# Moving the tail clears, the scatters, a table and the rank products of a fused attention, dense and routed kernel to other slots

## The chip, the cores and the metric

The kernel runs on one core of a Trainium2 chip. The metric is the device time of one execution in microseconds; three executions of the kernel before took 601.76, 603.11 and 604.13 us, median 603.11 us. One further execution was recorded by the hardware profiler, and all rows below come from it.

## What is computed

Three stages follow each other; the second and third work on 3072 tokens of 256 values.

```python
# 1. chunked linear attention, 4 x 8 heads, 768 positions, head 32, state 16
y[:, :, sl] = y_intra + y_inter
# 2. dense layer 256 -> 2048 -> 256 with a leaky relu per hidden column
h = x @ w_in
g = np.maximum(h, 0.0) + alpha * np.minimum(h, 0.0)
x = g @ w_out
# 3. eight experts 256 -> 1024 -> 256, the best one of each token
logits = x @ w_gate + modality_bias[modality_id]
e_idx = np.argmax(logits, axis=1)
for e in range(E):
    mask = e_idx == e
    h = np.maximum(x[mask] @ w1[e], 0.0)
    out[mask] = gate_w[mask, None] * (h @ w2[e])
```

## The kernel before

The tokens are cut into nine blocks of 2 or 3 chunks of 128 (`SIZES`). Attention makes the input of a block, the dense layer takes it through 16 units of 128 hidden columns, and routing sends its rows to their experts: they are scattered into a table `srt` in DRAM that has one stretch of rows for each expert. The expert stage then takes 14 items; an item is one page of 256 rows of one expert (`xr`, read from `srt`) with that expert's weights (four loads of 512 KB, `raw`).

From block 3 on the work is written out by hand in **slots**, under `manual_schedule`, so that each engine takes its instructions in the order in which the slots issue them. Blocks 3 to 8 have 16 slots each, then each item has 8. `at[k, f]` is the slot of unit f of block k, and `ui` is the first slot of item 0, which comes right behind slot 15 of block 8, the last block. In slot u PE makes the first product of unit u (`ph`, six matmuls), ACT and DVE make `t` and `g` from it, ACT and POOL split the `g` of slot u-1 into `gh` and `gl` (L616, L618), and PE makes the second product (`px`) of the unit of slot u-4 (`LAG`), which needs that unit's `gh` and `gl`. `g` has three buffers, the PSUM tile `ph` three. The table `todo` hangs everything else on slots with `do(slot, function)`:

- **Routing** of a block, `route_at`: `route_mm` and `route_act` (logits and rows, `pxr`, `xr`), `route_b`, `route_exp`, `route_gate`, `route_c` (the ranks of the tokens within their experts, products `pr` on PE) and `route_d` (L553: adds the running count `cnt`, makes the row numbers `pi`, and issues one indirect DMA for each chunk, L569, on POOL's queue: the **scatter**). For blocks 0 to 2 `pr` lies in one of the three `ph` tiles.
- **Tails**: `tail_counts` (L1012) copies `cnt` to `cnti` on DVE and calls `clear_tails` (L457): eight DMAs on SP's queue, one for each expert, each writes 640 empty rows of 1032 bytes behind the expert's last row so far, 8 x 660 KB in all. Only the last block's scatters are told to come behind them (L576 to L578); scatters of other blocks lie behind nothing, since no clear stands ahead of them in the program.
- **Tables**: `item_tables` (L716 to L742 and above) works out which item has which expert and page, on DVE, in four steps of a slot each. Table 0 serves items 0 and 1, table 1 (`tab_194`) items 2 to 8, table 2 the rest. `item_load` reads the table and loads the weights, `item_rows` loads the page behind all scatters and clears so far; both issue on SP's queue, in program order.

A scheduler adds the semaphores: an instruction waits for the earlier ones whose data it reads or overwrites, unless `declare_no_dep` says that two don't meet. A scatter writes to rows that only data tells, so it counts as a write to the whole of `srt`.

Of the kernel before, what the change touches and what calls it, by code (L numbers as in the profile page):

```python
# [112 lines left out]
def ssm_moe_moe_kernel(  # L113
# [26 lines left out]
    blocks = [(sum(SIZES[:k]), n) for k, n in enumerate(SIZES)]  # L140
# [57 lines left out]
    blk = {}  # L198
# [160 lines left out]
    m2p = []  # L359
# [189 lines left out]
    def wait_for(i, o, why):  # L549
        tc.add_manual_dep(i, o.name, mybir.DependencyInfo(mybir.DependencyClass.Sync, mybir.DependencyReason.DATA),  # L550
                          reason=why)

    def route_d(k):  # L553
        c0, n = blocks[k]
        d = blk[k]
        pr, oh, xr = d["pr"], d["oh"], d["xr"]
        sh = [P, n, NE]
        V = nc.vector

        q = small.tile([P, MX, NE], F32, tag="q", name="q")  # L560
        V.tensor_tensor(q[:, :n], pr[:, :n], cnt[:, None, :].to_broadcast(sh), ALU.add)
        V.tensor_tensor(cnt, pr[:, n], cnt, ALU.add)
        V.tensor_tensor(q[:, :n], q[:, :n], oh[:, :n], ALU.mult)
        pf = small.tile([P, MX], F32, tag="pf", name="pf")
        V.tensor_reduce(pf[:, :n], q[:, :n], AX.X, ALU.add)
        pi = small.tile([P, MX], I32, tag="pi", name="pi")
        V.tensor_copy(pi[:, :n], pf[:, :n])
        for t in range(n):
            sc = nc.gpsimd.indirect_dma_start(  # L569
                out=srt[:, :], out_offset=bass.IndirectOffsetOnAxis(ap=pi[:, t:t + 1].bitcast(U32), axis=0),  # L570
                in_=xr[:, t, :ROW], in_offset=None, bounds_check=NROW - 1, oob_is_err=False)

            for o in scat:
                tc.declare_no_dep(sc.ins, o, reason="rows are disjoint")
            scat.append(sc.ins)
            if k == len(blocks) - 1:  # L576
                for o in tails:
                    wait_for(sc.ins, o, "rows behind the last ones")  # L578
# [366 lines left out]
    split_load(1)  # L945
    for step in (route_a, route_b, route_exp, route_gate, route_c, route_d):
        step(0)

    last = len(blocks) - 1
    slots = [("m",) + q for q in late] + [("i", i, fc) for i in range(NSTATIC) for fc in range(KF2)]
    at = {q[1:]: u for u, q in reversed(list(enumerate(slots))) if q[0] == "m"}
    ui = len(late)
# [3 lines left out]
    def do(u, fn, *args):  # L958
        todo.setdefault(u, []).append((fn, args))
# [65 lines left out]
    def route_at(k, mms, b):  # L1025
        for t, u in enumerate(mms):
            do(u, route_mm, k, t)
            do(u + 1, route_act, k, t)
        for v, fn in zip(b, (route_b, route_exp, route_gate, route_c, route_d)):
            do(v, fn, k)  # L1030

    u = at[NS, 0]
    route_at(1, (u, u + 1), (u + 4, u + 5, u + 6, u + 6, u + 8))
    route_at(2, (u + 5, u + 7), (u + 9, u + 10, u + 11, u + 11, u + 14))
    for k in range(NS, last + 1):
        u = at[k, 15] + 1
        if k < last - 1:
# [4 lines left out]
    def table_at(u, j, pool):  # L1042
        steps = []

        def step():
            if not steps:
                steps.append(item_tables(j, pool[-1]))
            next(steps[0], None)

        for v in range(u, u + 5):  # L1050
            do(v, step)

    table_at(at[last - 1, 14], 0, small_)
    table_at(at[last, 11], 1, m2p)
    do(ui, tail_counts)
    table_at(ui + 12, 2, m2p)

    for k in range(NS, last):
        c0, n = blocks[k + 1]
# [3 lines left out]
        for j in range(n):  # L1063
            c, b = c0 + j, at[k, 0] + 5 * j - (k > NS)
# [30 lines left out]
    for i in range(2, NSTATIC):  # L1095
        b = ui + KF2 * (i - 2)
# [109 lines left out]
```

## Time and profile before

| | us |
|---|---|
| median of three executions | 603.11 |
| the profiled execution | 600.14 |
| its span from first to last instruction | 598.3 |
| PE busy in the span | 549.2 (92%) |
| DVE busy | 437.9 (73%) |
| ACT busy | 319.0 (53%) |
| POOL busy | 242.0 (40%) |
| mean granted TensorE clock | 0.95 of 2.4 GHz |

PE is busy all through most 15 us windows; the windows in which it isn't are the start (up to 180 us, where blocks 0 to 2 run with their attention) and two around the change from the dense layer to the items, 405 to 450 us. Idle time of another engine counts only where PE waits for it. A row of the timeline gives the start in us, the length in us, engine and line, the operation with its tiles, how many were merged, and in brackets the idle time before it and what ended that.

### The profile page before, as it was taken

The numbers are of one execution on the slowest core, as the hardware profiler recorded it, in microseconds if no ns is written. First come the engines' busy times: TensorE is split into PE (matmuls) and PEld (weight loads), VectorE is DVE, ScalarE is ACT, GpSimd is POOL, SyncE is SP. The second block draws the span as 40 slices with busy tenths as digits, with TensorE's granted clock in tenths as the row PEclk, the third lists the DMA queues.
The fourth block names the chain that finished last, engine by engine and source line by source line (L and its number), as shares of the span: only waits on it lengthen the run. The fifth ranks groups of instructions, "written<-read, shape, count | busy, mean of one in ns | idle before, by whom it ended". The sixth has DMA issues, their size and how long they took to land. (4 is left out here: it accounts for less than half of the span.)

```text
span 598.3 us, 12098 instructions
## 1 busy us (share of the span) xinstructions
PE 549.2 (92%) x4271; PEld 515.5 (86%) x4271; DVE 437.9 (73%) x861; ACT 319.0 (53%) x702; POOL 242.0 (40%) x258
## 2 busy tenths in 40 slices
PE   7988785999879999989999999997959999999993
PEld 7867575799768899979999999997959999999993
DVE  4998797963787777778766777488549777877860
ACT  0563664565564354464444444564537677767761
POOL 1143353655435654845845746454004122211211
PEclk9785797999999999999999999997979999999998
DMA  7977654520145226225234200631997976777400
GB/s 231 285 256 222 208 179 148 167 89 1 36 135 171 96 85 182 78 86 180 92 101 145 84 24 22 204 134 35 276 315 248 331 242 218 214 233 230 144 25 7
DMA packets 60563, 92.15 MB, mean 154 GB/s; under 512 B 5102, under 2 KB 37040, under 8 KB 60496
## 3 DMA queue, kind: packets, MB, share of 16 engines
q1 hardware_dynamic: 56974, 82.83, 44.3%
q0 software_dynamic: 2400, 6.32, 2.9%
q10 hardware_dynamic: 1122, 2.16, 1.3%
q8 instruction: 36, 0.59, 0.4%
q14 instruction: 31, 0.25, 0.2%
HBM read 75.59 MB, written 15.96 MB: 153 GB/s over the span
## 5 line engine op out<-in xcount | busy, mean ns | idle before, releaser
L618 POOL TENSOR_TENSOR gl<-g,gh 128x384 fp32r<-128x384 f32 (+1 forms) x144 | 146.8, 1023 | 147.0 <-ACT gh L616 144.6
L607 ACT ACTIVATE t<-ph,sgn 128x384 f32<-128x384 f32 (+1 forms) x144 | 78.5, 546 | 121.2 <-PE ph L153 105.2
L609 DVE SCALAR_TENSOR_TENSOR g<-ph,sal,t 128x384 f32<-128x384 f32 (+1 forms) x144 | 81.1, 566 | 69.8 <-ACT t L607 69.0
L153 PE MATMUL ph<-xh,wi_h 128*128 128x384 f32 (+1 forms) x288 | 100.0, 349 | 14.6 <-DVE g L609 14.4
L153 PE MATMUL px<-gl,wo_h 128*128 128x384 f32 (+1 forms) x288 | 94.9, 330 | 1.7 <-POOL gl L618 1.7
L153 PE MATMUL px<-gh,wo_h 128*128 128x384 f32 (+1 forms) x288 | 94.6, 329 | 1.8 <-ACT wo_h L424 1.4
L153 PE MATMUL px<-gh,wo_l 128*128 128x384 f32 (+1 forms) x288 | 94.0, 327 | 0.0
L153 PE MATMUL ph<-xl,wi_h 128*128 128x384 f32 (+1 forms) x288 | 93.1, 324 | 0.3 <-DVE xl L159 0.3
L153 PE MATMUL ph<-xh,wi_l 128*128 128x384 f32 (+1 forms) x288 | 93.0, 323 | 0.0
L616 ACT CAST gh<-g 128x384 fp32r<-128x384 f32 (+1 forms) x144 | 67.4, 469 | 17.3 <-DVE g L609 17.1
L877 POOL DMA_INDIRECT out_dram<-ob,xr x26 | 28.1, 1080 | 111.3 <-ACT ob L876 65.9
L153 PEld LDWEIGHTS ph<-xh,wi_h 128*128 128x128 f32 x288 | 55.6, 194 | 19.9 <-DVE g L609 16.7
L854 ACT ACTIVATE rh<-ph 128x256 fp32r<-128x256 f32 (+1 forms) x112 | 41.6, 371 | 54.0 <-PE ph L153 53.2
L855 DVE SCALAR_TENSOR_TENSOR rl<-ph,rh 128x256 fp32r<-128x256 f32 (+1 forms) x112 | 45.2, 403 | 23.5 <-ACT rh L854 22.5
L153 PEld LDWEIGHTS px<-gl,wo_h 128*128 128x128 f32 x288 | 56.4, 196 | 3.2 <-POOL gl L618 2.1
L153 PEld LDWEIGHTS px<-gh,wo_h 128*128 128x128 f32 x288 | 56.7, 197 | 2.3 <-ACT wo_h L424 1.6
L153 PEld LDWEIGHTS px<-gh,wo_l 128*128 128x128 f32 x288 | 56.5, 197 | 0.2 <-DVE wo_l L159 0.2
L153 PEld LDWEIGHTS ph<-xl,wi_h 128*128 128x128 f32 x288 | 55.9, 194 | 0.8 <-DVE xl L159 0.5
L153 PEld LDWEIGHTS ph<-xh,wi_l 128*128 128x128 f32 x288 | 55.8, 194 | 0.0
L153 PE MATMUL ph<-x2h,wi_h 128*128 128x256 f32 x144 | 41.7, 290 | 5.6 <-DVE rl L855 5.6
L964 DVE TENSOR_TENSOR_SCAN ab<-ab,id 128x512 f32<-128x512 f32 x30 | 44.2, 1475 | 0.0
L569 POOL DMA_INDIRECT srt<-xr,pi x24 | 25.7, 1072 | 43.5 <-DVE sets L695 30.5
(149 smaller groups left out, 1306.5 us busy)
## 6 DMA issues: line engine op xcount, KB each, us to landing
raw<-in_w_dram SPq DMA_DIRECT2D x56, 512.0 KB
ab<-a_scr SPq DMA_DIRECT2D x24, 512.0 KB
srt<-zr SPq DMA_DIRECT2D x8, 645.0 KB
raw<-in_w_in_dram SPq DMA_DIRECT2D x8, 512.0 KB
raw<-in_w_out_dram SPq DMA_DIRECT2D x8, 512.0 KB
bs<-bcs SPq DMA_DIRECT2D x38, 96.0 KB
bs<-bcs SPq DMA_DIRECT2D x19, 192.0 KB
xr<-srt SPq DMA_DIRECT2D x14, 258.0 KB
```

The lines of the kernel that those rows point to most:

```text
L153: nc.tensor.matmul(o, l, r, start=start, stop=stop)
L569: sc = nc.gpsimd.indirect_dma_start(out=srt[:, :], out_offset=bass.IndirectOffsetOnAxis(ap=pi[:, t:t + 1].bitcast(U32), axis=0), in_=xr[:, ...
L607: nc.scalar.activation(t[:, :N], ph[:, :N], AF.Copy, scale=sg)
L609: nc.vector.scalar_tensor_tensor(g[:, :N], ph[:, :N], sal[:, fc:fc + 1], t[:, :N], ALU.mult, ALU.max)
L616: nc.scalar.copy(gh[:, :N], g[:, :N])
L618: nc.gpsimd.tensor_tensor(gl[:, :N], g[:, :N], f(gh[:, :N]), ALU.subtract)
L854: nc.scalar.activation(rh[:, :n], ph[:, :n], AF.Relu)
L855: nc.vector.scalar_tensor_tensor(rl[:, :n], ph[:, :n], 0.0, f(rh[:, :n]), ALU.max, ALU.subtract)
L877: nc.gpsimd.indirect_dma_start(out=out[:, :], out_offset=bass.IndirectOffsetOnAxis(ap=xr[:, t, ROW - 1:ROW].bitcast(U32), axis=0), in_=ob, ...
L964: nc.vector.tensor_tensor_scan(lt[:, s_].rearrange("p h i -> p (h i)"), lt[:, s_].rearrange("p h i -> p (h i)"), id8[:, s_].rearrange("p h ...
```

## The change

- `route_d` no longer issues the scatters. They are a function of their own, `route_out(k, ts)`. For blocks 1 to 7 the scatters of a block are issued one a slot, in the three (or two) slots behind `route_d`; for block 8 in `route_d`'s own slot, as before. Block 0's all go out at once, as before.
- `tail_counts` moves from slot `ui` to slot `at[8, 11]`, five slots earlier. In that slot it is issued behind the first scatter of block 7, and ahead of the other two (slots 12 and 13).
- Table 1 starts at `at[8, 13]` and not at `at[8, 11]`.
- For blocks 1 and 2 `route_c` comes a slot later, `route_d` too.

```diff
-        for t in range(n):
+        d["pi"] = pi
+
+    def route_out(k, ts):
+        pi, xr = blk[k]["pi"], blk[k]["xr"]
+        for t in ts:
             sc = nc.gpsimd.indirect_dma_start(
                 out=srt[:, :], out_offset=bass.IndirectOffsetOnAxis(ap=pi[:, t:t + 1].bitcast(U32), axis=0),
                 in_=xr[:, t, :ROW], in_offset=None, bounds_check=NROW - 1, oob_is_err=False)
@@
     for step in (route_a, route_b, route_exp, route_gate, route_c, route_d):
         step(0)
+    route_out(0, range(blocks[0][1]))
@@
+        n = blocks[k][1]
+        if k < last:
+            for t in range(n):
+                do(b[-1] + 1 + t, route_out, k, (t,))
+        else:
+            do(b[-1], route_out, k, range(n))
+
     u = at[NS, 0]
-    route_at(1, (u, u + 1), (u + 4, u + 5, u + 6, u + 6, u + 8))
-    route_at(2, (u + 5, u + 7), (u + 9, u + 10, u + 11, u + 11, u + 14))
+    route_at(1, (u, u + 1), (u + 4, u + 5, u + 6, u + 7, u + 9))
+    route_at(2, (u + 5, u + 7), (u + 9, u + 10, u + 11, u + 12, u + 15))
@@
-    table_at(at[last, 11], 1, m2p)
-    do(ui, tail_counts)
+    table_at(at[last, 13], 1, m2p)
+    do(at[last, 11], tail_counts)
```

POOL's queue in block 8 before: the three scatters of block 7 (they write `srt_80` by the row numbers `pi_5271`) and the splits `gl` around them, with the semaphores that each waits for (HW are SP's and ACT's DMAs, SW POOL's own).

```order
L618 TENSOR_TENSOR gl_5243<-g_5214,gh_5241 128x384 [waits PE_49,Activation_49]
L569 DMA srt_80<-xr_5056,pi_5271 26880x258 [waits DMAHW2_49,DMAHW7_49,DMASW2_49,DVE_49]
L569 DMA srt_80<-xr_5056,pi_5271 26880x258 [waits DMASW3_49]
L569 DMA srt_80<-xr_5056,pi_5271 26880x258 [waits DMASW4_49]
L618 TENSOR_TENSOR gl_5297<-g_5239,gh_5295 128x384 [waits PE_49,Activation_49]
L618 TENSOR_TENSOR gl_5326<-g_5293,gh_5324 128x384 [waits PE_49,Activation_49]
L618 TENSOR_TENSOR gl_5352<-g_5322,gh_5350 128x384 [waits PE_49,Activation_49]
```

The same place of POOL's queue in the changed kernel; `gl_5288`, `gl_5395`, `gl_5421` are the splits of units 10, 11 and 12.

```order
L622 TENSOR_TENSOR gl_5288<-g_5239,gh_5286 128x384 [waits PE_49,Activation_49]
L573 DMA srt_80<-xr_5056,pi_5271 26880x258 [waits DMAHW2_49,DMAHW7_49,DMASW2_49,DVE_49]
L622 TENSOR_TENSOR gl_5395<-g_5284,gh_5393 128x384 [waits PE_49,Activation_49]
L573 DMA srt_80<-xr_5056,pi_5271 26880x258 [waits DMAHW7_49,DMASW3_49]
L622 TENSOR_TENSOR gl_5421<-g_5391,gh_5419 128x384 [waits PE_49,Activation_49]
L573 DMA srt_80<-xr_5056,pi_5271 26880x258 [waits DMASW4_49]
L622 TENSOR_TENSOR gl_5458<-g_5417,gh_5456 128x384 [waits PE_49,Activation_49]
```

The three scatters stood in a row between units 9 and 10 and stand now between units 10 and 13, one behind each split, and the second has one more semaphore to wait for, DMAHW7. In the built program the value that it waits for there is the one that the eighth tail clear sets (each of the eight uses one of DMAHW0 to DMAHW7 in turn).

DVE at the end of block 8 before: the last step of table 1 (`va`, `tf`, `tab`), `x2l` of item 0 (the input that PE needs for the first unit of item 0), and the copy `cnti` that starts the clears.

```order
L609 SCALAR_TENSOR_TENSOR g<-ph,sal,t 128x384
L738 SCALAR_TENSOR_TENSOR va<-rk,cst 128x192
L741 TENSOR_REDUCE tf<-va 128x2
L742 CAST tab_194<-tf 128x2
L838 TENSOR_TENSOR x2l<-pt,x2h 128x512
L609 SCALAR_TENSOR_TENSOR g<-ph,sal,t 128x384
L159 TENSOR_TENSOR wi_l<-raw_5070,wi_h 128x2x256
L855 SCALAR_TENSOR_TENSOR rl<-ph_5423,rh 128x256
L1013 CAST cnti<-cnt 128x8
```

DVE in the changed kernel, from the `g` of unit 11 on, five slots ahead of that.

```order
L613 SCALAR_TENSOR_TENSOR g<-ph,sal,t 128x384
L1018 CAST cnti<-cnt 128x8
L159 TENSOR_TENSOR w2l<-raw_5018,w2h 128x512
L613 SCALAR_TENSOR_TENSOR g<-ph,sal,t 128x384
L159 TENSOR_TENSOR w2l<-raw_5020,w2h 128x512
L613 SCALAR_TENSOR_TENSOR g<-ph,sal,t 128x384
L699 SCALAR_TENSOR_TENSOR sets<-cnt,cst 128x96 x2
L708 TENSOR_TENSOR sets<-sets 128x96
L709 TENSOR_TENSOR sets<-sets 128x96
L720 SCALAR_TENSOR_TENSOR rk<-cst,sets 128x288
L159 TENSOR_TENSOR w2l<-raw_5020,w2h 128x512
L613 SCALAR_TENSOR_TENSOR g<-ph,sal,t 128x384
```

`cnti` now follows the `g` of unit 11, and the table's first step (`sets`) comes behind the `g` of unit 13. The table's last two steps now stand behind `x2l` and behind the `g` of unit 15. On SP's queue the order is as before: the loads of items 0 and 1, the eight clears, the load of item 2; the read of table 1 ahead of that load now has a wait of its own for DVE.

## Rows read from the trace of the kernel before

**Rows 1.** Windows of 15 us: busy us of PE, PEld, DVE, ACT, POOL; clock, DMA share, GB/s.
```profile
405.00:420.00 15.00, 11.28 (x54) 10.76 (x53) 12.19 (x21) 5.70 (x12) 5.98 (x6) 0.77 0.17 59
435.00:450.00 15.00, 8.79 (x69) 8.29 (x68) 7.67 (x27) 6.39 (x17) 2.17 (x2) 0.77 1.06 324
450.00:465.00 15.00, 15.00 (x130) 15.00 (x129) 13.53 (x31) 10.55 (x25) 5.05 (x5) 1.00 0.76 252
```
**Rows 2.** Timeline of PE where item 0 starts (slot `ui`).
```profile
409.15 0.34 PE L153 MATMUL px<-gl,wo_h 128*128 128x384 f32 x1
...
413.59 0.58 PE L153 MATMUL ph<-x2l,w1h 128*128 128x256 f32 x1 [2.48 <-DVE x2l L838]
...
415.46 0.52 PE L153 MATMUL px<-gl,wo_h 128*128 128x384 f32 x1
...
419.30 0.38 PE L153 MATMUL px<-gh,wo_l 128*128 128x384 f32 x1
```
**Rows 3.** Timeline of DVE, slots 11 of block 8 to 1 of item 0.
```profile
400.85 0.61 DVE L609 SCALAR_TENSOR_TENSOR g<-ph,sal,t 128x384 f32<-128x384 f32 x1
...
404.21 3.71 DVE L725 TENSOR_TENSOR rk<-rk,sets 128x288 f32<-128x288 f32 x1
...
412.86 0.68 DVE L838 TENSOR_TENSOR x2l<-pt,x2h 128x512 fp32r<-128x512 f32 x1
...
415.88 0.16 DVE L1013 CAST cnti<-cnt 128x8 int32<-128x8 f32 x1
```
**Rows 4.** Timeline of POOL, from the last scatter of block 7 on.
```profile
403.39 1.23 POOL L569 DMA_INDIRECT srt<-xr,pi  x1 [0.30 <-issue]
404.64 2.96 POOL L618 TENSOR_TENSOR gl<-g,gh 128x384 fp32r<-128x384 f32 x3
...
447.52 0.99 POOL L569 DMA_INDIRECT srt<-xr,pi  x1 [30.53 <-DVE sets L695]
```
**Rows 5.** Timeline of SP's queue: clears, weights of item 2, rows of item 2.
```profile
416.89 12.33 SPq L461 DMA_DIRECT2D srt<-zr  x8
430.33 5.20 SPq L784 DMA_DIRECT2D raw<-in_w_dram  x4
440.22 0.38 SPq L791 DMA_DIRECT2D xr<-srt  x1
```
**Rows 6.** Waits of SP's queue, 428 to 456 us: total, times, longest.
```profile
SPq L791 <- DMA srt<-zr: 3.7, 2, 2.4
```
**Rows 7.** Windows while the clears move; columns as in rows 1, the last is GB/s.
```profile
418.00:420.00 2.00, 2.00 (x11) 2.00 (x10) 1.12 (x2) 0.89 (x2) 0.00 (x0) 0.66 1.02 342
418.00:430.00 12.00, 11.62 (x85) 11.39 (x84) 6.33 (x14) 7.00 (x16) 0.00 (x0) 0.94 1.07 291
432.00:440.00 8.00, 5.46 (x53) 5.22 (x51) 1.61 (x9) 0.76 (x2) 0.00 (x0) 0.99 1.09 232
440.00:440.50 0.50, 0.00 (x0) 0.00 (x0) 0.00 (x0) 0.00 (x0) 0.00 (x0) 0.50 1.05 389
```
**Rows 8.** Timeline of PE around slot 8 of the items.
```profile
437.18 0.28 PE L153 MATMUL px<-w2h,rl 128*128 128x256 f32 x1
443.10 0.58 PE L153 MATMUL ph<-x2h,wi_h 128*128 128x256 f32 x1 [5.64 <-DVE rl L855]
...
447.02 0.37 PE L153 MATMUL ph<-x2h,wi_h 128*128 128x256 f32 x1
```
**Rows 9.** Timeline of ACT around slot 8 of the items.
```profile
433.45 0.37 ACT L499 COPY xr<-pxr 128x256 f32<-128x256 f32 x1 [0.77 <-DVE L L498]
441.37 0.62 ACT L816 CAST wi_h<-raw 128x512 fp32r<-128x512 f32 x1 [7.55 <-DMA raw<-in_w_dram]
```
**Rows 10.** Timeline of PE around block 1's rank products.
```profile
176.34 0.44 PE L153 MATMUL ph<-xh,wi_h 128*128 128x384 f32 x1 [2.06 <-DVE g L609]
...
180.90 0.44 PE L153 MATMUL ph<-xh,wi_h 128*128 128x384 f32 x1 [0.17 <-DVE g L609]
```
**Rows 11.** Timeline of ACT there.
```profile
179.55 0.58 ACT L607 ACTIVATE t<-ph,sgn 128x384 f32<-128x384 f32 x1 [0.67 <-ACT part L1007]
```

More of the change, by code (lines that the diff above doesn't have):

```diff
@@ L555, in route_d @@
         d = blk[k]
-        pr, oh, xr = d["pr"], d["oh"], d["xr"]
+        pr, oh = d["pr"], d["oh"]
         sh = [P, n, NE]
```

## The prediction

> **What bounds the kernel now.** I read the windows of 15 us first [rows 1]. PE is the only engine that is ever full for long: 15.00 of 15 us from 450 on, and likewise from 185 to 405. Where it is full, an edit on another engine is worth nothing. It isn't full at the start, and in 405 to 420 (11.28) and 435 to 450 (8.79), where the granted clock is 0.77 besides. So I looked at these places in the timelines of PE, DVE, POOL and SP's queue.
>
> **Gap A**, start of item 0 [rows 2]: the last product of slot 15 starts at 409.15. After it PE does a single product before it waits 2.48 us for DVE's `x2l`, until 413.59. The cause is on DVE [rows 3]: one addition of table 1 took 3.71 us where it started beside POOL's scatter and three splits `gl` that POOL had in arrears [rows 4]; the table's last operations stood ahead of `x2l` too. When PE comes back the products of 384 columns take 0.52 us, at half clock (1.2 GHz), until 419.30. A product `px` that reads `gl` of unit 12 starts at 415.46; without the gap that would be about 410.4 (409.15 and some seven products). Gap A costs 415.46 - 410.4 = 5.1 us, and the slow phase behind it 3.84 us at half speed, so 1.92: 7.0 us.
>
> **Gap B**, some 28 us behind the start of item 0 [rows 8]: PE does nothing from 437.46 to 443.10, then runs at half clock to about 447. ACT had waited 7.55 us, until 441.37, for the weights `raw` of item 2 [rows 9]. These loads stood on SP's queue behind the clears: clears issued from 416.89 over 12.33 us, weights from 430.33 [rows 5]. A product takes 0.115 us where PE is full (15.00 us by 130 [rows 1]); PE did some 16 between 437.18 and 447.02, so the gap costs 9.84 - 1.84 = 8.0 us, taken as 7.9 since the first of them was one of the old run.
>
> **The change part by part.**
>
> *Ranks of blocks 1 and 2 a slot later.* In block 1 `pr` takes a `ph` bank and the first product of the next unit waits 2.06 us for `g`; one unit on it waits only 0.17 more [rows 10], and the ACT operation that ends that second wait starts at 179.55 behind `part` work [rows 11] that the change leaves where it is. In the changed order `pr` itself takes the later wait. The earlier wait goes, the later one grows. I take +0.5 us, from -1 (half of the 2.06 saved) to +2 (another wait of 2.06).
>
> *Scatters of blocks 1 to 7, one a slot.* POOL's own work is the same, 1 us for each scatter. In blocks 3 to 6 PE is full, and `px` comes four units behind `gl`'s `g`: 0. In block 7 the three no longer stand in a row, so POOL has no arrears of three splits and gap A's first cause is gone. But this is also where the tails come in.
>
> *Tails five slots earlier.* `cnti` follows the `g` of unit 11, which starts at 400.85 [rows 3], so at about 401.5. The first clear followed `cnti` by 416.89 - 415.88 = 1.0 us; now it does so at 402.4. The order shows a new wait: the second scatter of block 7 waits for DMAHW7, which the eighth clear sets, since the clears now stand ahead of it in the program and both write `srt`. **Queued behind it on POOL** are the `gl` of units 12 to 15 and the third scatter. POOL takes its queue in order: in the kernel before it stood idle 30.53 us at a scatter of the last block [rows 4]. Waiting for them: PE, which needs `gl` of unit 12 for the third product `px` of slot `ui`; and DVE, whose `g` of unit 15 needs the buffer that `gl` of unit 12 gives back (`g` has three). Behind that `g` stand the end of table 1 and so SP's load of item 2. `x2l`, `x2h` and the first unit of item 0 aren't behind it.
>
> How long is the wait? The clears' time from first issue to last landing, D, isn't a row; it is bounded. SP's load of item 2's rows waits for the clears (3.7 us in two waits [rows 6]) and goes out at 440.22, so D is at most 440.1 - 416.89 = 23.2 us. What the queues move is 342 GB/s in the first two us, 291 in the mean of 418 to 430, and 232 from 432 to 440, then 389 when only weights remain [rows 7]. The wait says that they end near 439.3 to 440.1, less up to 1.8 us for weights (0.42 MB at 232) that may have moved between: D is 21.4 to 23.2, and I take 22.4. If the clears went at 291 GB/s throughout, 5.28 MB would take 18.2 us, and D would be 19.2 with the 1.0 to the first transfer; at 342 GB/s 16.4. The slow rate of 232 fell in a stretch where the clears themselves were what remained, so I take the high value and keep 19.2 as the lower bound of the range's forecast.
>
> By the queue, then, the second scatter may start at 402.4 + 22.4 = 424.8, takes 1.0 (the row of 0.99 in [rows 4]), `gl` of unit 12 takes another 1.0 (three in 2.96), and with 0.2 for the semaphore PE goes on at 427.0. Before, the same product started at 415.46: **+11.5 us** (8.3 with D of 19.2, 5.5 with 16.4, 12.3 with 23.2). PE's stall is about 16.6 us long, from 410.4; it replaces gap A, and does not come on top.
>
> After the stall PE starts at half clock again. That phase lasted 413.59 to 419.30, 5.7 us [rows 2], and 443.10 to 447.02 at most, 3.9 us [rows 8]: it loses half of it, 2.85 or 1.95, where the kernel before lost 1.92 behind 415.46. **+0.4** (0 to +0.9).
>
> *Item 2's weights.* SP is free of clears long before, so the load goes out when table 1 is done, some 7 to 8.5 us behind 424.8: about 432, and takes under 8 (a load alone runs at 389 GB/s [rows 7], 2 MB in 5.4 us): landed by 440. ACT needs them 11.5 us later than it did before (433.82, the end of the copy in [rows 9]), at 445. So gap B goes, **-7.9** (0 if the weights are late after all, which is a rival).
>
> *Table 1 two slots later.* It frees DVE ahead of `x2l`, which gains nothing as PE waits for `gl` by then. When POOL comes back it does four splits and a scatter in a row, and DVE's table step stands beside them; in [rows 3] one such step took 3.71 us where others take under 1. **+0.3** (0 to +1).
>
> **The sum**: +11.5 + 0.4 - 7.9 + 0.3 + 0.5 = **+4.8 us**. The profiled execution took 600.14 (span 598.3, 1.84 around it), so the changed kernel's profile would be at 604.9. The median of the runs, 603.11, lies 3 us above the profile; on its level the change gives **607.9 us**. The lower ends together: 8.3 + 0 - 7.9 + 0 - 1 = -0.6, 602.5; the upper: 12.3 + 0.9 - 7.9 + 1 + 2 = +8.3, 611.4.
>
> **The rivals.**
>
> *The wait doesn't hold PE* (the scatter is covered, or the clears are not what it waits for). Then gap A and gap B both go: -7.0 - 7.9 + 0.5 = -14.4, 588.7 us. For it speaks that this is what the edit lets free; against it that the order shows the wait and POOL's queue behind it, and that the 30.53 us row shows POOL standing still at such a wait. It decides if `gl` of unit 12 is done by 410.4, that is if D is under 6 us: no rate in [rows 7] allows that. Chance 0.08.
>
> *The clears are quick where nothing else loads.* At 342 GB/s D is 16.4: +5.5 + 0.4 - 7.9 + 0.3 + 0.5 = -1.2, 601.9 us. For it: no weights of items move in 402 to 425 in the new place, and the first two us ran at 342. Against it: in 418 to 430 no weights moved either, and the mean was 291. Chance 0.12 (0.10 within 0.5%, 0.02 faster). The Trainium skill, "DMA: Bandwidth & Descriptors", section "Specifications", bears on this: it gives about 358 GB/s to one core from HBM, and line rate for pieces of 512 bytes and more, which a row of 1032 bytes is; by that page D would be an estimated 14.7 + 1.0 us and the sum about -1.8. The rows of 291 and 232 GB/s disagree with it.
>
> *Item 2 is late all the same*: table 1 stands behind DVE's `g` of unit 15, the load behind that, and if the four splits and `g`s come slower than I assume, or the load shares the queues, the weights land after ACT asks. Then gap B stays and only the stall is added: +11.5 + 0.4 + 0.3 + 0.5 = +12.7, 615.8 us. It decides if the load goes out after about 437 (445 less 8). Against it: 5 us of slack. Chance 0.10, all slower.
>
> **How the numbers follow.** The forecast has 0.70. About 0.5% of the time, 3.0 us, is what a measurement of this kernel can tell from no change; of the forecast's own range of -0.6 to +8.3 the part above +3.0 holds most, D of 21 to 23 being the likelier: 0.58 slower, 0.12 the same. Faster: 0.08 + 0.02 = 0.10. Same: 0.12 + 0.10 = 0.22. Slower: 0.58 + 0.10 = 0.68. The range holds the forecast and the quick clears, 601.9 to 611.5, 0.8 in all; the late weights and the free PE lie outside.
>
> **What would show it.** Right: POOL idle some 20 us before the second scatter of block 7; the first clear near 402 and the last landing near 425; PE waiting for `gl` of unit 12 from about 410 to 427, at half clock after; no wait of ACT for `raw` of item 2 about 28 us into the items; item 2's load issued near 432; in block 1 no wait at `pr`'s old place and one still near 180.9. Wrong: a stall of PE much shorter than 16 us (D was too long), POOL not standing at the scatter, or ACT waiting for `raw` again.

## The result

The changed kernel takes 611.18 us (median of four runs, 609.36 to 613.64); the kernel before, in the same four rounds, 603.62 (601.76 to 605.31). The ratio is 1.0129, 95% interval 1.0081 to 1.0176: slower by some 7.8 us (1.29% of 603.62; the medians themselves lie 7.6 apart). The forecast was 607.9 with 601.9 to 611.5: slower, as forecast, and near the top of the range. The profiled execution took 611.05, span 609.3, 11.0 more than the profiled one of before; why that is more than 7.8 is told below.

The windows of 15 us of the changed kernel, columns as in [rows 1] (PE, PEld, DVE, ACT, POOL, clock, DMA share, GB/s):

```profile
405.00:420.00 15.00, 11.28 (x67) 10.65 (x65) 9.72 (x24) 7.86 (x16) 3.43 (x3) 0.94 0.78 198
420.00:435.00 15.00, 1.64 (x5) 1.64 (x6) 1.66 (x2) 1.01 (x2) 3.51 (x4) 0.50 0.64 173
435.00:450.00 15.00, 14.62 (x102) 14.38 (x101) 12.47 (x27) 7.41 (x18) 2.43 (x3) 0.88 0.55 185
```

The hole of [rows 1] in 435 to 450 is filled (14.62 us of PE, where it was 8.79), and a larger one stands ahead of it: 1.64 us in 420 to 435. PE's timeline there, against [rows 2]:

```profile
415.32 0.39 PE L153 MATMUL ph<-x2l,w1h 128*128 128x256 f32 x1 [0.26 <-DVE x2l L842]
...
433.36 0.69 PE L153 MATMUL px<-gl,wo_h 128*128 128x384 f32 x1 [16.83 <-POOL gl L622]
433.85 0.52 PE L153 MATMUL px<-gh,wo_h 128*128 128x384 f32 x1
...
438.43 0.40 PE L153 MATMUL ph<-x2h,w1l 128*128 128x256 f32 x1
438.65 0.30 PE L153 MATMUL ph<-x2h,w1h 128*128 128x256 f32 x1
```

PE hardly waits for `x2l` now (0.26 us for 2.48), but 16.83 us for `gl` of unit 12, and then runs at 1.2 GHz until 438.6. POOL (against [rows 4]) says why:

```profile
407.42 1.33 POOL L573 DMA_INDIRECT srt<-xr,pi  x1 [0.15 <-DVE cnti L1018]
408.79 1.01 POOL L622 TENSOR_TENSOR gl<-g,gh 128x384 fp32r<-128x384 f32 x1
431.28 0.99 POOL L573 DMA_INDIRECT srt<-xr,pi  x1 [21.48 <-DMA srt<-zr]
432.30 1.01 POOL L622 TENSOR_TENSOR gl<-g,gh 128x384 fp32r<-128x384 f32 x1
```

The second scatter of block 7 stood 21.48 us until a clear (`srt<-zr`) had landed, and the split that PE wanted stood behind it. SP's queue, against [rows 5]:

```profile
408.15 12.99 SPq L461 DMA_DIRECT2D srt<-zr  x8
440.58 2.27 SPq L788 DMA_DIRECT2D raw<-in_w_dram  x4
```

From the first clear's issue to the scatter's start are 431.28 - 408.15 = 23.1 us. Four windows within them (columns as above):

```profile
421.00:427.00 6.00, 0.00 (x0) 0.00 (x0) 0.00 (x0) 0.00 (x0) 0.00 (x0) 0.50 1.10 286
427.00:431.00 4.00, 0.00 (x0) 0.00 (x0) 0.00 (x0) 0.00 (x0) 0.00 (x0) 0.50 0.41 103
429.00:430.00 1.00, 0.00 (x0) 0.00 (x0) 0.00 (x0) 0.00 (x0) 0.00 (x0) 0.50 0.09 28
430.00:431.00 1.00, 0.00 (x0) 0.00 (x0) 0.00 (x0) 0.00 (x0) 0.00 (x0) 0.50 0.00 0
```

All compute engines stand. The DMA engines move 286 GB/s until 427; after that the rate falls, to 28 GB/s in 429 to 430 and to nothing in 430 to 431. So the clears' bytes have all moved more than 1 us before the scatter goes, and the mean of 103 GB/s over the last 4 us is no steady rate.

### The profile page after: what moved, and what is told of

Its sections match the earlier page's. It is cut to its first block, busy times and chain, and to the rows that moved or that the text cites. A ratio compares the mean times of both kernels' runs of the same rounds, so it can differ in the third digit from the quotient of the medians.

```text
span 609.3 us, 12098 instructions
## 1 busy us (share of the span) xinstructions
PE 549.0 (90%) x4271; PEld 514.2 (84%) x4271; DVE 438.7 (72%) x861; ACT 319.1 (52%) x702; POOL 239.0 (39%) x258
## 5 line engine op out<-in xcount | busy, mean ns | idle before, releaser
L622 POOL TENSOR_TENSOR gl<-g,gh 128x384 fp32r<-128x384 f32 (+1 forms) x144 | 142.9, 995 | 151.7 <-ACT gh L620 149.2
L573 POOL DMA_INDIRECT srt<-xr,pi x24 | 28.4, 1184 | 47.7 <-DMA srt<-zr 21.5
```

The source lines that it names most:

```text
L573: sc = nc.gpsimd.indirect_dma_start(out=srt[:, :], out_offset=bass.IndirectOffsetOnAxis(ap=pi[:, t:t + 1].bitcast(U32), axis=0), in_=xr[:, ...
L622: nc.gpsimd.tensor_tensor(gl[:, :N], g[:, :N], f(gh[:, :N]), ALU.subtract)
```

## What was tried

Two questions are open after this: is the POOL wait all of it, and where do the other microseconds come from, since the whole kernel runs 5.45 us late already before slot 8 of block 8? To place a loss, I took the start of each of the 144 `t<-ph` operations (and of each `rl<-ph` in the items) in two traces, and followed the difference. PE's, DVE's and ACT's instructions stand in the same order in all these kernels up to about 154 us; what differs up to there is no effect of an edit. In that stretch the profiled execution of the kernel before was ahead of every other one by 0.2 to 3.7 us (of the changed kernel by 2.37), so I count only what comes behind it. **Late** below is the start of such an operation less the start of the same one in the kernel before.

**The wait alone.** The changed kernel, but block 7's scatters declared to be apart from the clears:

```diff
-            for o in scat:
+            for o in scat + (tails if k < len(blocks) - 1 else []):
                 tc.declare_no_dep(sc.ins, o, reason="rows are disjoint")
```

> The changed kernel with block 7's later scatters declared to be apart from the tail clears (their rows lie ahead of the clears' rows), so that the second scatter has no clear to wait for; all else as changed. Theory (the wait on POOL holds PE): POOL's idle time of 21.48 us goes, PE goes from block 8 into item 0 without a stop, gap A and most of gap B go; against the kernel before -7.0 -7.9 +0.5, with up to 5 us back if the weights of item 2, 2 MB behind 5.28 MB of clears, land late (needed near 427): 589 to 596 us. Rival 1 (the clears' traffic beside the last slots is what slows, whoever waits for it): above 603. Rival 2 (most of the loss lies ahead, in blocks 1 and 2): near 600.

596.58 us, ratio 0.9909 (0.9877 to 0.9940). One dependency is thus worth some 13 us (1.0129 less 0.9909), and the clears' traffic shows no cost of its own: while they move, PE stays 5.66 us late from unit 11 to unit 14 of block 8 (rival 1 falls). But it is slower than the 588.7 that the prediction gave for this case: gap A shrank only by 1.6 us (5.66 late before it, 4.02 behind it). PE at the start of item 0, and DVE ahead of it:

```profile
418.85 0.58 PE L153 MATMUL ph<-x2l,w1h 128*128 128x256 f32 x1 [3.58 <-DVE x2l L842]
```
```profile
411.04 1.76 DVE L699 SCALAR_TENSOR_TENSOR sets<-cnt,cst 128x96 f32<-128x96 f32 x2
...
413.43 1.93 DVE L720 TENSOR_TENSOR_SCAN rk<-cst,sets 128x288 f32<-128x288 f32 x1
...
416.87 1.33 DVE L732 TENSOR_TENSOR rk<-rk 128x96 f32<-128x96 f32 x2
418.12 0.68 DVE L842 TENSOR_TENSOR x2l<-pt,x2h 128x512 fp32r<-128x512 f32 x1
```

In the changed kernel, where POOL stood still at that time, the same three are

```profile
410.81 0.41 DVE L699 SCALAR_TENSOR_TENSOR sets<-cnt,cst 128x96 f32<-128x96 f32 x2
...
411.85 0.76 DVE L720 TENSOR_TENSOR_SCAN rk<-cst,sets 128x288 f32<-128x288 f32 x1
...
414.11 0.55 DVE L732 TENSOR_TENSOR rk<-rk 128x96 f32<-128x96 f32 x2
```

With POOL at work beside them they take 5.02 us and not 1.72. In place of the one operation of 3.71 us in [rows 3] three are longer by 0.8 to 1.4 us each, and beside each of them POOL has a single split of 1.0 us.

**The rest without the clears.** The changed kernel with `tail_counts` back in slot `ui`:

> The changed kernel with the tail clears back in slot ui; scatters spread, table 1 later, ranks later as changed. Theory: no scatter of block 7 waits, gap A goes (-7.0) as POOL's arrears and the table are out of the way, gap B stays since the weights are again behind the clears, with the clears some 5 us earlier as they hang on the slot: 596 to 600 us. Rival 2 (the ranks' move and the spread scatters cost more than the theory's 0.5 ahead of block 3): 600 to 605. Rival 1 says as the theory here.

608.17 us, ratio 1.0092 (1.0057 to 1.0126): slower than the kernel before, and outside what every theory had said. The trace shows both gaps in place (PE waits 3.50 us for `x2l`; ACT waits 10.82 for `raw`), and a loss far ahead of them: 3.3 us between 154 and 205 us and 1.1 near 258. What the shorter gap A gave, 3.1 us, the longer gap B took back (3.3), as PE came to the same late weights sooner.

**The clears alone.** The kernel before with `do(at[last, 11], tail_counts)`; there the three scatters of block 7 stand ahead of the clears.

> The kernel before with one edit: tail clears in at[8, 11], where all three scatters of block 7 stand ahead of them in the program. Theory: no new wait on POOL; gap A stays (DVE's step of 3.71 us beside POOL's arrears), gap B goes as the clears are through before item 2's weights are wanted: 603 - 7.9 = about 595 us. Rival 1 (clears' traffic costs in itself): 603 or more.

593.9 us, ratio 0.9863 (0.9835 to 0.9892): 8.2 us faster, where -7.9 had been worked out for gap B. At gap A PE waits 2.48 us for `x2l` as in [rows 2], and 1.32 us for ACT's `x2h` just ahead of that (1.23 in the kernel before, a wait that the prediction did not name); ACT never waits for `raw`. Nothing is lost between 154 and 258 us.

**Half the wait.** The changed kernel with four clears in `at[8, 11]` and four in slot `ui`:

> The changed kernel with four of the eight clears issued in at[8, 11] and four in slot ui. On the queue they follow each other as before, but the second scatter of block 7 now waits for the fourth clear and not the eighth. Theory: the wait is the clears' own time, so half the clears halve it: POOL idle about 10 us in place of 21.48, PE back about 11 us earlier, 600 to 601 us. Rival 1 (traffic): as the changed kernel, 611. Rival 2: as the theory here.

602.93 us (1.0022, 1.0006 to 1.0038): by the two ratios 6.5 us faster than the changed kernel, and in the traces 8.4 from block 8's slot 8 on. Its time lies 2 us above the 600 to 601 expected. The order on SP's queue is the same, and only the clear that the scatter waits for is another. SP's queue, then POOL, then PE:

```profile
410.04 12.87 SPq L461 DMA_DIRECT2D srt<-zr  x8
```
```profile
424.41 0.99 POOL L573 DMA_INDIRECT srt<-xr,pi  x1 [12.69 <-DMA srt<-zr]
```
```profile
426.48 0.69 PE L153 MATMUL px<-gl,wo_h 128*128 128x384 f32 x1 [8.04 <-POOL gl L622]
```

POOL's wait falls by 8.8 us and PE's by 8.8 (16.83 to 8.04): one for one. The scatter went 14.4 us after the first issue and not at half of 23. The likely reason, not tested, is that the eight clears overlap: SP issues the later four from 416.6 on, before the fourth has landed.

**The ranks alone.** The kernel before with `route_c` and `route_d` of blocks 1 and 2 a slot later:

> The kernel before with one edit: route_c and route_d of blocks 1 and 2 a slot later. In the traces so far PE's order up to about 154 us is the same, and from there to 205 us the kernels with the ranks later and the scatters spread lose 2.1 to 3.3 us, the kernel with the clears alone moved loses nothing. Theory E1 (the ranks' place does it: pxr waits 1.38 us for xr and ph 2.18 us for g): +2 us against the kernel before, with the 258 us stretch untouched. Theory E2 (the spread scatters of blocks 0 to 2 do it, by POOL beside DVE): 0 +- 0.5.

604.94 us, ratio 1.0041 (1.0011 to 1.0071). The trace loses 3.1 us between 154 and 205 us (from 1.41 late to 4.54) and nothing more until item 0. (Behind item 0 it loses a further 1.4, where nothing had been moved; by the ratio the edit costs 2.5 in all.) The 3.1 us are two losses: 2.0 until 198, behind block 1's ranks, and 1.1 near 205, behind block 2's. PE at the first:

```profile
175.27 0.40 PE L153 MATMUL ps<-bs 128*128 128x128 bf16 x4 [1.96 <-DVE xl L159]
...
179.37 0.73 PE L153 MATMUL pxr<-idwg,xT 128*128 128x136 f32 x4 [1.39 <-ACT xr L499]
182.28 0.69 PE L153 MATMUL ph<-xh,wi_h 128*128 128x384 f32 x1 [2.18 <-DVE g L609]
182.77 0.52 PE L153 MATMUL ph<-xl,wi_h 128*128 128x384 f32 x1
...
187.25 0.52 PE L153 MATMUL ph<-xh,wi_h 128*128 128x384 f32 x1
```

The earlier wait of 2.06 us [rows 10] is gone. The product that stands at 180.90 in [rows 10] now starts at 182.28. The 1.38 us between them are the 1.41 that the trace was late already: this wait ends at the same point of ACT's chain, as the prediction had it. What follows differs. In the kernel before PE came to that wait already at half clock, having done its slow products (0.52 us each, from 177 to 180) while it had to wait for ACT anyway, and was at full clock behind it:

```profile
178.18 0.52 PE L153 MATMUL px<-gh,wo_l 128*128 128x384 f32 x1
...
181.19 0.34 PE L153 MATMUL ph<-xl,wi_h 128*128 128x384 f32 x1
...
183.63 0.44 PE L153 MATMUL ph<-xh,wi_h 128*128 128x384 f32 x1 [0.34 <-DVE g L609]
```

Now the unit is done at full clock ahead of the wait, PE idles, and the half clock falls on the 5 us behind it (182.77 to 187.57): some 16 products at 0.32 us from one to the next and not 0.175, which is 2.3 us. Of these 0.34 fall into the wait that the kernel before had at 183.63; the trace shows 2.0. In the changed kernel the slow phase at this place ended sooner, at 185.97, and cost 1.0.

The second loss is a plain wait. PE at the first unit of block 4, and DVE, here and, behind that, in the kernel before:

```profile
208.08 0.44 PE L153 MATMUL ph<-xl,wi_h 128*128 128x384 f32 x1 [1.14 <-DVE xl L159]
```
```profile
206.41 0.17 DVE L561 TENSOR_TENSOR q<-pr,cnt 128x16 f32<-128x16 f32 x1
...
207.51 0.17 DVE L567 CAST pi<-pf 128x2 int32<-128x2 f32 x1
207.60 0.42 DVE L159 TENSOR_TENSOR xl<-py,xh 128x256 fp32r<-128x256 f32 x1
```
```profile
199.35 0.17 DVE L561 TENSOR_TENSOR q<-pr,cnt 128x16 f32<-128x16 f32 x1
...
200.46 0.17 DVE L567 CAST pi<-pf 128x2 int32<-128x2 f32 x1
202.47 0.62 DVE L609 SCALAR_TENSOR_TENSOR g<-ph,sal,t 128x384 f32<-128x384 f32 x1 [1.84 <-ACT t L607]
203.07 0.42 DVE L159 TENSOR_TENSOR xl<-py,xh 128x256 fp32r<-128x256 f32 x1
```

Block 2's `route_d`, five short operations, stood in a slot in which DVE then waited 1.84 us for ACT anyway. A slot later it stands straight ahead of `xl`, which PE needs for the first unit of block 4, and PE waits 1.14 us. The changed kernel's trace has the same wait, 1.14 us at 208.08.

**The scatters alone.** The kernel before with the scatters of blocks 1 to 7 one a slot:

> The kernel before with the scatters of blocks 1 to 7 one a slot, and nothing else. Theory E1: blocks 1 and 2 as before; +1.2 us near 258 us, where one DVE subtraction took 2.67 us and not 1.21 in the kernels with spread scatters; in block 8 table 1's step of 3.71 us falls apart into several that are each about 1 us longer, so gap A stays: +1 to +2 us. Theory E2: +3.3 us or more. Had the prediction's reading of gap A been right (three splits in arrears), gap A would go: -4 or so.

601.73 us, ratio 0.9972 (0.9943 to 1.0001), hardly a difference. Several things nearly cancel. Near 258 us 1.1 us are lost on DVE's subtraction of `rbc`, which runs beside POOL's `gl`, `bd`, `gl` in a row:

```profile
256.12 2.66 DVE L159 TENSOR_TENSOR rbc<-rbc,part 48x1024 f32<-48x1024 f32 x1
```
```profile
252.74 1.21 DVE L159 TENSOR_TENSOR rbc<-rbc,part 48x1024 f32<-48x1024 f32 x1
```

(ahead the spread kernel, behind it the kernel before). The first `rbc` took 2.66 or 2.67 us in all six traces with every scatter spread, and 1.20 or 1.21 in the six others. And gap A shrinks by 3.8 us (4.16 late before it, 0.36 behind it): one wait of 2.67 us is left, PE goes on from it at full clock, and ACT's `x2h` is in time. Of this 0.8 are lost again at gap B and 0.9 in the items behind it.

**Table 1 behind `x2l`.** Clears in `at[8, 11]`, scatters in a row, table 1 from `at[8, 13]`, and then from `at[8, 15]` with item 2's load two slots later:

> The kernel before with two edits: tail clears in at[8, 11] and table 1 from at[8, 13] on; block 7's scatters in a row ahead of the clears. Compared with the clears alone moved (593.9 us, 0.986 of the kernel before). Theory A1 (POOL's scatters and splits in a row hold whichever DVE operation stands beside them, so that DVE is late for x2l whatever it does there): no better than 0.986. Theory A2 (the table's operations ahead of x2l are the load): half of them stand behind x2l now, so 1 to 3 us better.

593.36 us, ratio 0.9860 (0.9807 to 0.9912): as with the clears alone, which is what theory A1 said. PE waits 4.38 us for `x2l`.

> As the run before it, with table 1 from at[8, 15] on, so that all of it stands behind x2l; the load of item 2 two slots later, behind the table. Theory A2: x2l is in time, gap A goes, 4 to 7 us better than the clears alone moved (593.9), unless item 2's weights, issued some 4 us later, come late (needed near 430). Theory A1: 0 to 2 us better.

590.01 us, ratio 0.9783 (0.9729 to 0.9837), the best median but one, and by the ratios 4.8 us better than the clears alone, as theory A2 said. Only with all of the table behind `x2l` gap A nearly closes (0.94 us). POOL and DVE ahead of it:

```profile
407.07 3.94 POOL L618 TENSOR_TENSOR gl<-g,gh 128x384 fp32r<-128x384 f32 x4
```
```profile
408.13 0.62 DVE L609 SCALAR_TENSOR_TENSOR g<-ph,sal,t 128x384 f32<-128x384 f32 x1 [1.93 <-POOL gl L618]
408.67 2.90 DVE L159 TENSOR_TENSOR w2l<-raw,w2h 128x512 fp32r<-128x512 f32 x1
```

While POOL does four splits in a row, `g`, which reads one input from PSUM (`ph`), takes its usual 0.62 us; `w2l`, with both inputs in SBUF, takes 2.90 and not 0.69. The Trainium skill says in "GPSIMD Engine Reference", section "1. Specifications", that GpSimd shares its SBUF interfaces with VectorE, and that instructions of VectorE with two SBUF inputs contend for them; these two rows agree. Which operation is held depends on which one comes up beside POOL's splits: it was `rk` in [rows 3], `sets` in the run without the wait, `rbc` near 258 us and `w2l` here. The row of `g` shows a second way in which POOL's row of work holds DVE: it waited 1.93 us for a `gl`, which gives back one of the three buffers of `g`.

**Two more.** The fastest so far with block 7's scatters spread as well, apart from the clears; and the changed kernel without the wait and without the ranks' move:

> Clears in at[8, 11], table 1 from at[8, 15], item 2's load behind it (as the fastest run so far, 0.978), and block 7's scatters alone spread over slots 11 to 13 and declared apart from the clears. Theory (POOL's three scatters and four splits in a row hold a DVE operation of 0.69 us for 2.90 us ahead of x2l; spread, each hold is about 1 us shorter in sum): PE's wait for x2l of 0.94 us goes, 0.5 to 2 us faster than 0.978. Rival (the same POOL work holds DVE as long in pieces): the same as 0.978.

589.36 us, ratio 0.9805 (0.9772 to 0.9838). PE's wait for `x2l` is gone altogether, but the time is that of table 1 from `at[8, 15]`: the interval covers both, so a gain of under 2 us can't be told. The trace shows where the 0.9 us gained at gap A went: ACT now waits 1.98 us for item 2's weights, which it did not in that run.

```profile
430.73 0.62 ACT L822 CAST wi_h<-raw 128x512 fp32r<-128x512 f32 x1 [1.98 <-DMA raw<-in_w_dram]
```

> The changed kernel with block 7's scatters declared apart from the clears and the ranks of blocks 1 and 2 in their old slots. If the parts add up: 0.9909 (with the ranks moved) less 0.0041 to 0.005 for the ranks, 0.986 to 0.987, 594 to 595 us. If not (a loss ahead of a later wait is swallowed by it): 0.991 as with the ranks moved.

593.2 us, ratio 0.9874 (0.9845 to 0.9904), where 0.9909 less 0.0041 is 0.9868: the parts add up, and the 0.991 of the other case lies outside.

## Why the prediction held, step by step

- **The stall, +11.5 us.** The product with `gl` of unit 12 starts at 433.36 and not 415.46, 17.9 later, of which 5.45 is the lateness that the kernel had anyhow: +12.5. PE's wait is 16.83 us for 16.6 forecast. The row of 30.53 us in [rows 4], on which the prediction leaned, was a wait for DVE; that a clear holds POOL at a scatter is shown by the row of 21.48 us here. DVE stood at the `g` of unit 15 for 18.08 us, as the prediction had it. The clears' time D was taken as 22.4 between 21.4 and 23.2, and is 23.1 up to the scatter's start. The four-clear run shows that PE's wait follows POOL's one for one; the run without the dependency and the clears alone show no other cost of the clears' place.
- **Half clock, +0.4.** From 433.36 to 438.65, 5.3 us, so 2.65 lost for 1.92 in the kernel before: +0.7, within its bounds.
- **Item 2's weights, -7.9.** ACT has no wait for `raw`, and from the `rl` of slot 3 of item 0 to that of slot 1 of item 1 the lateness falls from 18.85 to 11.01 us: -7.84. The load went out at 440.58 and not near 432, since besides the 5.45 us a step of table 1 on DVE took 3.63 us at 433.88 beside POOL's scatter and splits; there was slack enough.
- **What is left of the items' part**: 11.0 - 5.45 = +5.55 for the +4.3 that these terms and DVE's +0.3 made. The mechanism held; of the 1.25 too little the stall has 1.0 and the half clock 0.3.
- **The ranks, +0.5.** Mis-sized: +2.2 in the changed kernel's trace (2.37 us late at 154, 4.53 at 205), 3.1 in the trace of the ranks alone, 0.7 to 4.3 by that run's interval. In block 1 the later wait did end on ACT's chain, and the earlier one brought nothing, as the prediction said. Two steps failed. It counted waits only: the half clock that follows a pause was hidden behind a wait before and stands open now, 1.0 us here and 2.0 in the run of the ranks alone. For the start of item 0 this term had been counted; for block 1 it had not. And block 2 was not priced at all: its `route_d` came to stand ahead of `xl`, and PE's wait for that made the other 1.1.
- **The spread scatters, 0 in blocks 3 to 6.** Wrong by +1.1 to 1.2 near 258 us, in each of the six traces with all of them spread; 0.2 to 0.3 of it came back in block 8. PE is full there, but by little: a DVE operation held 1.45 us longer was enough.
- **Gap A's cause.** The prediction laid it to three splits in arrears, one held operation and the table ahead of `x2l`; on the reading that all of it goes the rival without the stall was priced at 588.7. The run put it at 0.9909, 597.6 on the prediction's level. Of these 8.9 us the trace shows 5.4 at gap A, which shrank by 1.6 and not by 7.0, and some 2.6 at the ranks and the scatters. In single traces, with the slow phases as they fell, both causes count: the scatters spread alone took 3.8 us off gap A, the whole table behind `x2l` with the scatters in a row 4.8, and both 5.8. Half of the table behind `x2l`, with the scatters in a row, took nothing. The forecast did not hang on this, as PE waited for `gl` by then.
- **Quick clears.** That rival fell: 5.28 MB in 23.1 us. The bytes began about 1.0 us behind the first issue and ended more than 1 us before the scatter, so even the time in which they moved, some 20.5 us, gives only about 260 GB/s. The estimate of 15.7 us from the Trainium skill's "DMA: Bandwidth & Descriptors", section "Specifications", doesn't describe these clears.

The forecast's terms make +4.8, the trace behind 154 us 8.6 (11.0 less the 2.37 from a stretch where no instruction had moved), the medians 7.6. By the trace the shortfall is 3.9: 1.7 at the ranks, 0.9 at the scatters and 1.25 in the items' part. All the errors of any size point the same way, and 8.6 would lie just above the range's own upper sum of +8.3; the range held by the medians, and narrowly. The direction was no luck: the stall alone, +12.5, outweighs the -7.84 of item 2's weights.

## What to carry to other kernels

When a DMA that is issued earlier moves ahead of another that writes to the same tensor, look for the semaphore that this makes, for the engine whose queue takes it, and for everything in line behind it: here one needless order between rows that never meet cost some 13 us, more than the move itself could gain. If the rows are known to be apart, say so, or issue the small writers first; the same clears in the same slot behind the scatters made the kernel 1.4% faster. Price a pause of PE with its half clock: in block 1 a slow phase that ended in the next wait cost nothing, and the same phase behind the last wait cost 1.0 to 2.0 us. Not every pause brings one: behind the wait of 2.67 us in the run of the scatters alone PE went on at full clock. And where an edit moves several blocks, price each: block 2's small operations cost as much as block 1's pause.

## What the chip showed beside

A DVE operation with both inputs in SBUF stretches while POOL's splits run: 0.69 to 2.90 us beside four splits, 1.21 to 2.66 beside a run of three POOL operations. An operation with an input in PSUM did not (0.62). Two tensor inputs are not needed for it: `knw`, which reads one tensor, took 0.20 us in the kernel before and here

```profile
433.88 3.63 DVE L736 TENSOR_SCALAR knw<-rk 128x96 f32<-128x96 f32 x1
```
```profile
433.48 0.99 POOL L573 DMA_INDIRECT srt<-xr,pi  x1 [0.17 <-issue]
434.49 2.94 POOL L622 TENSOR_TENSOR gl<-g,gh 128x384 fp32r<-128x384 f32 x3
```

In these rows the held operation waits out POOL's whole run of splits, not one split: it ends 0.08 us behind the last split here, 0.56 in the row of `w2l` and 0.32 in [rows 3], each time its usual length (0.20, 0.69, 0.45) less 0.12 to 0.13.

And a set of eight clears of 660 KB took longer than its bytes: none moved in the last 1.3 us before the scatter that waited for them.
